# A spectral layer with an MLP: the second product as seven block products, on one core

## The chip, the cores and the metric

One Trainium2 chip, one of its cores. The metric is device microseconds from the start to the end of one execution. TensorE multiplies matrices into PSUM (eight banks), VectorE (DVE), ScalarE (ACT) and GpSimd (POOL) work element by element, SyncE (SP) and ScalarE issue the DMAs.

## What is computed

Eight sequences of 3008 tokens with 256 features pass through a Fourier layer and then through an MLP. Cut to what matters:

```
X  = rfft(x, axis=1)
Yr = Xr @ w_r - Xi @ w_i + b_r ;  Yi = Xr @ w_i + Xi @ w_r + b_i
soft threshold of both by 0.01
y  = irfft(Y)                                # 24064 tokens of 256 features
h  = y @ w_in                                # 256 -> 2048
g  = maximum(0.01 * h, h)                    # leaky relu
out = g @ w_out                              # 2048 -> 256
```

The MLP's weights arrive as float64. Their products are to be more accurate than a single pass of TensorE on the rounded type (float32r) gives, so each operand is split in a high and a low part, and a product is three matmuls: high x high, low x high, high x low.

## The kernel before

The transform length is 47 x 64. A batch passes through `fwd` (transform over n1, its result goes through DRAM as u_dram), `mid` (transform over n2 in `stage_b`, projection in `proj`, threshold, inverse over k2 in `stage_g`, result through DRAM as v_dram), and then, chunk by chunk, `inverse` (over k1) and the MLP. A chunk is two of the 8 x 13 (batch, s) sets and has up to 470 tokens; there are 52. For each chunk and each f (16 blocks of 128 of the 2048 hidden features) there is one step:

- `moe_h(ci, f)`: 6 matmuls of 470 columns (2 halves of the 256 features x 3 parts) into a psh bank (L76, the helper `products`); then L401 ACT 0.01 h into gf, L402 DVE maximum, L403 ACT copy to the high part gh, L404 DVE low part gl.
- `moe_o(ci, f)`: for each of two halves of the output 3 matmuls of 470 columns with w_out as the stationary operand, accumulated over the 16 f in a pso bank (L420). At the last f, L426 ACT copies the result to ob and SP writes it to DRAM.

`moe` writes the order: step f's first product, then the second product of the step three earlier (LAG = 3); v_load of the next chunk at f = 4, its inverse at f = 10 and 12. After each step the generators of `mid` for the next batch and `fwd` for the third after are advanced in proportion, so that they end at three quarters of a batch. The framework then orders the instructions of each engine by its own timeline, starting from that order, and sets the semaphores; tiles with one tag share their buffers, and one that finds none free waits for the release of an older one.

Before the MLP starts there is a prologue: `fwd` of three batches and `mid` of the first in plain float32, and `load_mlp`, which turns the float64 weights into high and low parts in 16 pieces of 512 elements per partition (8 of w_in, 8 of w_out). The last five pieces use buffers that the MLP doesn't need. PSUM: psh 2 banks, psf (transforms) 3, pso 3.

Of the kernel before, what the change touches and what calls it, by code (L numbers as in the profile page):

```python
# [10 lines left out]
U32 = mybir.dt.uint32  # L11
# [13 lines left out]
# High words of float64 numbers, read as float32: the last that float32 holds, and the one that becomes zero.  # L25
# [5 lines left out]
def spectral_mlp_kernel(  # L31
# [23 lines left out]
    NT = 2 * NG * N1  # L55
    CS = 512
    LAG = 3
    # Batches whose first stage runs before the MLP starts, without splitting its operands.
# [11 lines left out]
    def products(dst, pairs):  # L70
        """dst = sum of lhsT.T @ rhs over pairs of operands, each float32 or two parts of it."""
# [25 lines left out]
    def load_weights():  # L97
        """w_r, w_i - w_r and -(w_r + w_i)."""
        r = sb.tile([P, NH, D], F32, name="w_r", tag="yh")
        d = sb.tile([P, NH, D], F32, name="w_d", tag="yl")  # L100
        n = sb.tile([P, NH, D], F32, name="w_n", tag="gl", bufs=LAG + 1)
        i = sb.tile([P, NH, D], F32, name="w_i", tag="c", bufs=1)
# [13 lines left out]
    def float64_parts(src, dh, dl, tags):  # L116
# [3 lines left out]
        raw = sb.tile([P, CS, 2], U32, name="raw", tag=tags[0][0], bufs=tags[0][1])  # L120
# [3 lines left out]
        a = sb.tile([P, CS], F32, name="cva", tag=tags[1])  # L124
        q = sb.tile([P, CS], F32, name="cvq", tag=tags[2])
# [8 lines left out]
        av, qv = (t.rearrange("p (a f) -> p a f", a=na) for t in (a, q))  # L134
        act.copy(dh, av)
        pool.tensor_sub(av, av, dh.bitcast(F32))
        pool.tensor_add(dl, av, qv)

    def load_mlp():
        """Piece by piece; the last ones stay off the buffers that the MLP needs."""  # L140
        ih, il = pair("win", [P, NH, DF])
        oh, ol = pair("wout", [P, NF, D])
        iv, ov = (w.bitcast(U32).rearrange("(a p) f -> p a f", p=P) for w in (w_in, w_out))
        n = CS // NH
        pieces = []
        for c in range(DF // n):
            s = slice(c * n, (c + 1) * n)
            pieces.append((iv[:, :, 2 * c * n:2 * (c + 1) * n], ih[:, :, s], il[:, :, s]))
        n = CS // D
        for c in range(NF // n):  # L150
            s = slice(c * n, (c + 1) * n)
            pieces.append((ov[:, s, :], oh[:, s, :], ol[:, s, :]))
        for i, p in enumerate(pieces):
            early = i < len(pieces) - 5
            float64_parts(*p, (
                ("vin", 2) if early and i % 3 else ("raw", 1),
                ("xh", "xl")[i % 2] if early else "xh",
                ("ob", "gf")[i % 2] if early else "xl",
            ))
            yield 1  # L160

# [1 line left out]
    u_dram = {}  # L163
    first = []
    v_dram = {}
# [65 lines left out]
    def mid(b):  # L231
# [96 lines left out]
        for j in range(2):  # L328
            load(j)
# [288 lines left out]
```

## Time and profile before

| | before |
|---|---|
| median of 3 runs | 2721.57 us (2718.25 to 2722.91) |
| span of the profiled execution, first to last instruction | 2717.4 us |
| mean granted TensorE clock | 0.994 |
| TensorE busy, matmuls | 2662.3 us, 13810 |
| VectorE busy | 1818.5 us |
| ScalarE busy | 1407.4 us |
| GpSimd busy | 317.1 us |
| moved by DMA | 164.79 MB |

The profiled execution is given by its span; its time as the runs measure it is not listed apart. A profile line of a group reads: source line, engine, operation, output<-inputs, shapes, count | busy us, mean ns of one | idle time of the engine just before, and what ended it. "psh<-yh,win_hi" is a matmul into psh with win_hi as weights and yh as the moving operand. PEld are the weight loads, which lie beside the matmuls. Matmul durations overlap with one another.

### The profile page before, as it was taken

The numbers are of one execution on the slowest core, as the hardware profiler recorded it, in microseconds if no ns is written. First come the engines' busy times: TensorE is split into PE (matmuls) and PEld (weight loads), VectorE is DVE, ScalarE is ACT, GpSimd is POOL, SyncE is SP. The second block draws the span as 40 slices with busy tenths as digits, with TensorE's granted clock in tenths as the row PEclk, the third lists the DMA queues.
The fourth block names the chain that finished last, engine by engine and source line by source line (L and its number), as shares of the span: only waits on it lengthen the run. The fifth ranks groups of instructions, "written<-read, shape, count | busy, mean of one in ns | idle before, by whom it ended". The sixth has DMA issues, their size and how long they took to land.

```text
span 2717.4 us, 37211 instructions
## 1 busy us (share of the span) xinstructions
PE 2662.3 (98%) x13810; PEld 2376.7 (87%) x13810; DVE 1818.5 (67%) x3236; ACT 1407.4 (52%) x2779; POOL 317.1 (12%) x245
## 2 busy tenths in 40 slices
PE   6789999999999999999999999999999999999999
PEld 3568888988899888998889888999989999899888
DVE  5988776766767676766667766566656666555554
ACT  3455555555555555555555555555545555445454
POOL 3761110111110111110010100000000000000000
PEclk9899999999999999999999999999999999999999
DMA  8642222221221212221221211211111111100000
GB/s 265 193 146 79 70 57 67 63 58 54 59 62 56 60 56 56 78 59 49 64 60 54 65 53 38 63 36 46 41 46 42 38 34 30 41 30 14 15 15 14
DMA packets 122347, 164.79 MB, mean 61 GB/s; under 512 B 13757, under 2 KB 83381, under 8 KB 122165
## 3 DMA queue, kind: packets, MB, share of 16 engines
q1 hardware_dynamic: 78885, 111.27, 13.4%
q10 hardware_dynamic: 43280, 51.14, 7.1%
q8 instruction: 109, 1.79, 0.3%
q14 instruction: 73, 0.60, 0.1%
HBM read 86.59 MB, written 75.76 MB: 60 GB/s over the span
## 4 chain that ended last, share of the span: by engine, by line
PE 92%; DVE 4%; DMA 2%; issue 1%; ACT 1%; SPq 0%; POOL 0%; ACTq 0%; DVEq 0%
PE pso L420 38%; PE psh L76 38%; PE psf L76 10%; PE psf L373 3%; PE psf L258 3%; DVE t L301 1%; DMA u_dram<-xin 1%; DMA xin<-x_dram 0%; DVE t L303 0%; DMA raw<-w_out_dram 0%; DVE cva L129 0%; DVE cva L131 0%; DMA u<-u_dram 0%; DVE cva L130 0%; DVE raw L132 0%
## 5 line engine op out<-in xcount | busy, mean ns | idle before, releaser
L402 DVE TENSOR_TENSOR gf<-gf,psh 128x470 f32<-128x470 f32 (+1 forms) x832 | 529.3, 636 | 416.6 <-ACT gf L401 408.9
L404 DVE TENSOR_TENSOR gl<-gf,gh 128x470 fp32r<-128x470 f32 (+1 forms) x832 | 562.8, 677 | 355.0 <-ACT gh L403 344.7
L401 ACT ACTIVATE gf<-psh 128x470 f32<-128x470 f32 (+1 forms) x832 | 463.5, 557 | 583.8 <-PE psh L76 572.5
L403 ACT CAST gh<-gf 128x470 fp32r<-128x470 f32 (+1 forms) x832 | 482.4, 580 | 469.5 <-DVE gf L402 466.8
L76 PE MATMUL psh<-yh,win_hi 128*128 128x470 f32 (+1 forms) x1664 | 638.1, 383 | 1.2 <-DVE gf L402 0.9
L420 PE MATMUL pso<-gh,wout_lo 128*128 128x470 f32 (+1 forms) x1664 | 619.8, 372 | 0.0
L76 PE MATMUL psh<-yh,win_lo 128*128 128x470 f32 (+1 forms) x1664 | 619.4, 372 | 0.0
L76 PE MATMUL psh<-yl,win_hi 128*128 128x470 f32 (+1 forms) x1664 | 619.0, 372 | 0.1
L420 PE MATMUL pso<-gh,wout_hi 128*128 128x470 f32 (+1 forms) x1664 | 618.1, 372 | 0.0
L420 PE MATMUL pso<-gl,wout_hi 128*128 128x470 f32 (+1 forms) x1664 | 578.8, 375 | 0.0
L76 PEld LDWEIGHTS psh<-yh,win_lo 128*128 128x128 f32 x1664 | 313.4, 188 | 37.2
L420 PEld LDWEIGHTS pso<-gh,wout_lo 128*128 128x128 f32 x1664 | 312.7, 188 | 36.7
L420 PEld LDWEIGHTS pso<-gh,wout_hi 128*128 128x128 f32 x1664 | 313.1, 188 | 34.5
L76 PEld LDWEIGHTS psh<-yh,win_hi 128*128 128x128 f32 x1664 | 314.0, 189 | 33.4 <-DVE gf L402 2.9
L76 PEld LDWEIGHTS psh<-yl,win_hi 128*128 128x128 f32 x1664 | 316.1, 190 | 29.1 <-DVE yl L387 0.4
L420 PEld LDWEIGHTS pso<-gl,wout_hi 128*128 128x128 f32 x1664 | 308.9, 188 | 33.1 <-DVE gl L404 0.2
L293 POOL TENSOR_TENSOR kb<-bias,kc 128x512 f32<-128x512 f32 x84 | 113.0, 1345 | 1482.8 <-ACT kc L292 1318.3
L301 DVE TENSOR_TENSOR t<-psf,kb 64x256 f32<-64x256 f32 x384 | 161.8, 421 | 30.5 <-PE psf L76 26.2
L373 PEld LDWEIGHTS psf<-ga,vin 120*128 120x128 f32 x832 | 119.8, 191 | 10.1 <-DMA vin<-v_dram 2.2
L373 PE MATMUL psf<-ga,vin 120*128 120x128 f32 x832 | 123.4, 274 | 1.2 <-DMA vin<-v_dram 1.2
L189 POOL TENSOR_TENSOR xs<-xin,xin 120x512 f32<-120x512 f32 (+1 forms) x49 | 64.9, 1325 | 472.3 <-DMA xin<-x_dram 218.1
L258 PEld LDWEIGHTS psf<-fb,u 128*128 128x128 f32 x672 | 96.2, 191 | 13.9 <-ACT kc L292 3.5
(110 smaller groups left out, 2610.1 us busy)
## 6 DMA issues: line engine op xcount, KB each, us to landing
u<-u_dram SPq DMA_DIRECT2D x192, 128.0 KB, 2.8
v_dram<-v ACTq DMA_DIRECT2D x192, 128.0 KB, 2.5
xin<-x_dram SPq DMA_DIRECT2D x96, 240.0 KB, 3.1
u_dram<-xin ACTq DMA_DIRECT2D x96, 240.0 KB, 2.4
vin<-v_dram SPq DMA_DIRECT2D x96, 240.0 KB, 3.3
out_dram<-ob SPq DMA_DIRECT2D x88, 235.0 KB, 2.3
raw<-w_in_dram SPq DMA_DIRECT2D x8, 512.0 KB, 5.6
raw<-w_out_dram SPq DMA_DIRECT2D x8, 512.0 KB, 4.8
```

Source lines behind the costliest of these rows:

```text
L76: nc.tensor.matmul(dst, a, b, start=(i == 0), stop=(i == len(terms) - 1))
L189: eng.tensor_add(xs, xa, xb)
L258: nc.tensor.matmul(pv[:, dh, :, i, :], u[:, i, s], fbt[:, 0:k + 2:k + 1, :], start=True, stop=True)
L293: pool.tensor_add(kb, bias, kc.unsqueeze(1).broadcast_to([P, 2, D]))
L301: dve.tensor_add(t[64 * r:64 * (r + 1), i, :], ps_y[s, r * D:(r + 1) * D], kb[s, r, :])
L373: nc.tensor.matmul(py[:, o:o + P], vin[:, c, i, s], consts["ga"][:, c, :], start=True, stop=True)
L401: act.mul(gf[:, :n], ph[:, :n], SLOPE)
L402: dve.tensor_max(gf[:, :n], gf[:, :n], ph[:, :n])
L403: act.copy(gh[:, :n], gf[:, :n])
L404: dve.tensor_sub(gl[:, :n], gf[:, :n], gh[:, :n].bitcast(F32))
L420: nc.tensor.matmul(po[:, :n], a[:, f, s], r[:, :n], start=(f == 0 and j == 0), stop=(f == NF - 1 and j == 2),)
```

## The change

- `_chunks` pairs sets of equal size: 48 chunks of two halves of 235 tokens (padded to 236 columns) and 4 of two halves of 188. The leftover smaller sets of two batches make one chunk.
- A step is now a pair q of two f. The 2 x 2 blocks of g (two f, two halves of the tokens) and of w_out (two f, two halves of the output) are multiplied by seven block products in place of eight. For w_out the combinations are formed once, in the prologue (`load_wout`); for g in each step: 7 blocks g with three differences or sums, and their high and low parts.
- `moe_h` has 2 x 6 matmuls of 472 columns; `moe_o` 7 x 3 of 236. The seven accumulators take half a bank each, 4 banks in one buffer (tag acc); the transforms keep 2 banks (psf).
- The leaky relu is one ScalarE instruction (Prelu) from PSUM in place of one of ScalarE and one of VectorE.
- At a chunk's end the accumulators are copied by ScalarE (four) and VectorE (three), seven GpSimd additions form the four results, and four DMAs write them.
- The lag is one pair. `mid` has two stages of look-ahead in place of three and loads u one ahead. Many buffers are single (eh, el, xh, xl, zh, zl, t, v, vin), those of x two in place of three; the clipped values go to kb. The weight pieces use the buffers of g, gh and gl. `fwd` after the third batch splits and loads a piece after its matmuls, no longer before.

The core of the diff:

```diff
     def load_wout(c):
+        pool.tensor_add(w32, cv[:, 0, :], cv[:, 1, :])
+        a11, a21, a12, a22 = (wv[:, f, e * P:(e + 1) * P] for f in range(2) for e in range(2))
+        dve.scalar_tensor_tensor(s[:, 1], a21, -1.0, a22, ALU.mult, ALU.subtract)
+        dve.tensor_sub(s[:, 2], a11, a21)
+        dve.scalar_tensor_tensor(s[:, 3], s[:, 1], -1.0, a11, ALU.mult, ALU.subtract)
+        dve.tensor_sub(s[:, 0], a12, s[:, 3])
+        act.copy(oh[:, 0:2], wv[:, :, 0:P])
+        act.copy(oh[:, 6], a22)
+        act.copy(oh[:, 2:6], s)
+        pool.tensor_sub(ol[:, 0:2], wv[:, :, 0:P], oh[:, 0:2].bitcast(F32))
+        dve.tensor_sub(ol[:, 6], a22, oh[:, 6].bitcast(F32))
+        dve.tensor_sub(ol[:, 2:6], s, oh[:, 2:6].bitcast(F32))
...
     def moe_h(ci, q):
+        g = sb.tile([P, 7, TP], F32, name="g", tag="g")[:, :, :tp]
+        for i in range(2):
...
+            act.activation(g[:, 1:3] if i else g[:, 0:5:4], ph, AF.Prelu, alpha=SLOPE)
-        act.mul(gf[:, :n], ph[:, :n], SLOPE)
-        dve.tensor_max(gf[:, :n], gf[:, :n], ph[:, :n])
-        act.copy(gh[:, :n], gf[:, :n])
-        dve.tensor_sub(gl[:, :n], gf[:, :n], gh[:, :n].bitcast(F32))
+        act.copy(gh[:, 0:3], g[:, 0:3])
+        dve.tensor_sub(g[:, 3:5], g[:, 0:3:2], g[:, 4:5].broadcast_to([P, 2, tp]))
+        dve.tensor_add(g[:, 5], g[:, 2], g[:, 3])
+        dve.tensor_sub(g[:, 6], g[:, 1], g[:, 5])
+        act.copy(gh[:, 3:7], g[:, 3:7])
+        dve.tensor_sub(gl[:, 0:3], g[:, 0:3], gh[:, 0:3].bitcast(F32))
+        dve.tensor_sub(gl[:, 3:7], g[:, 3:7], gh[:, 3:7].bitcast(F32))
...
     def moe_o(ci, q):
+        if q == 0:
+            acc_t[ci] = ps.tile([P, 8, 256], F32, name="acc", tag="acc", bufs=1)
+        acc = acc_t[ci]
+        for j in range(7):
+            for i, (a, r) in enumerate(((wh, gh), (wl, gh), (wh, gl))):
                 nc.tensor.matmul(
+                    acc[:, j, :tp], a[:, q, j, :], r[:, j, :],
...
+        act.copy(pc[:, 0:4], acc[:, 0:4, :n])
+        dve.tensor_copy(pc[:, 4:7], acc[:, 4:7, :n])
+        for dst, x, y in ((5, 5, 0), (1, 1, 0), (4, 4, 5), (0, 4, 3), (3, 3, 5), (2, 2, 3), (6, 6, 4)):
+            pool.tensor_add(pc[:, dst], pc[:, x], pc[:, y])
+        for j, r in enumerate((1, 2, 6, 0)):
...
+            sync.dma_start(out[s, o:o + n], pc[:, r])
...
     def moe():
+        for i, (ci, q) in enumerate(steps):
+            moe_h(ci, q)
             if ci + 1 < nch:
+                if q == 2:
                     v_load(ci + 1)
+                if q in (5, 6):
+                    inverse(ci + 1, q - 5)
...
+            if i:
+                moe_o(*steps[i - 1])
```

More of the change, by code (lines that the diff above doesn't have):

```diff
@@ L133, in float64_parts @@
         pool.tensor_mul(q, q, wl.bitcast(F32))
[L134 to L137, printed above, removed]
-    def load_mlp():
[L141 to L159, printed above, removed]
+        return cv, raw
@@ L160, in load_mlp @@
+    def load_mlp():
+        pair("win", [P, NH, DF])
+        pair("wout", [P, NQ, 7, P])
+        for c in range(DF * NH // CS):
+            load_win(c)
+            yield 1
+        for c in range(NQ):
+            load_wout(c)
             yield 1
@@ L326, in stage_g @@
                 act.dma_start(vd[c, 2 * j:2 * j + 2, :N2, :].rearrange("k n d -> n k d"), v[c * N2:(c + 1) * N2])
-        for j in range(2):
-            load(j)
+        load(0)
         yield 0
-        for s in range(NPAIR + 2):
-            if s + 2 < NPAIR:
-                load(s + 2)
+        for s in range(NPAIR + 1):
+            if s + 1 < NPAIR:
+                load(s + 1)
+            if s:
+                yield from proj(s - 1)
             if s < NPAIR:
@@ L345, in spectral_mlp_kernel @@
     nch = len(chunks)
-    t0 = [sum(N1 * sum(n for _, _, n in c) for c in chunks[:i]) for i in range(nch + 1)]
-    y_t, v_t, g_t, o_t = {}, {}, {}, {}
+    t0 = [sum(2 * N1 * c[0][2] for c in chunks[:i]) for i in range(nch)]
+    y_t, v_t, g_t, acc_t = {}, {}, {}, {}
+    yf = const.tile([P, 2, TP], F32, name="y")
     def v_load(ci):
-        vin = sb.tile([PA, 2, 2, D], F32, name="vin", tag="vin")
+        vin = sb.tile([PA, 2, 2, D], F32, name="vin", tag="vin", bufs=1)
         (b, s, _), (b1, _, _) = chunks[ci]
@@ L360, in v_load, with columns @@
         v_t[ci] = vin
+    def columns(ci):
+        n = chunks[ci][0][2] * N1
+        return n, n + n % 2
     def inverse(ci, eh):
-        (_, _, n0), (_, _, n1) = chunks[ci]
-        m = n0 + n1
-        ne, n = m * NK1, m * N1
+        m = chunks[ci][0][2]
+        w = m * NK1
+        n, tp = columns(ci)
         vin = v_t[ci]
-        py = bank("psf", 3)
+        py = bank("psf", 2)
         s = slice(eh * P, (eh + 1) * P)
@@ L424, in moe_o @@
-            if f == NF - 1:
-                ob = sb.tile([P, NT], F32, name="ob", tag="ob")
-                act.copy(ob[:, :nt], po[:, :nt])
-                sync.dma_start(out[s, t0[ci]:t0[ci + 1]], ob[:, :nt])
-    steps = [(ci, f) for ci in range(nch) for f in range(NF)]
+                    acc[:, j, :tp], a[:, q, j, :], r[:, j, :],
+                    start=(q == 0 and i == 0 and j % 2 == 0), stop=(q == NQ - 1 and i == 2),
+                    skip_group_check=True,
+                )
+        if q < NQ - 1:
+            return
@@ L431, in moe @@
+    steps = [(ci, q) for ci in range(nch) for q in range(NQ)]
+    home = [c[1][0] for c in chunks]
     def moe():
-        for i, (ci, f) in enumerate(steps):
-            moe_h(ci, f)
-            if i >= LAG:
-                moe_o(*steps[i - LAG])
+        for i, (ci, q) in enumerate(steps):
+            moe_h(ci, q)
             if ci + 1 < nch:
-                if f == 4:
+                if q == 2:
                     v_load(ci + 1)
-                if f in (10, 12):
-                    inverse(ci + 1, (f - 10) // 2)
-            yield 2 * (ci + (f + 1) / NF) / NS
@@ L569, in _chunks, with n2 @@
 def _chunks(nb):
-    sets = [(b, s, NG if (NG - 1) * NS + s < N2 else NG - 1) for b in range(nb) for s in range(NS)]
-    assert len(sets) % 2 == 0
-    return [sets[i:i + 2] for i in range(0, len(sets), 2)]
+    def n2(s):
+        return NG if (NG - 1) * NS + s < N2 else NG - 1
+    full = [s for s in range(NS) if n2(s) == NG]
+    rest = [s for s in range(NS) if n2(s) < NG]
+    assert len(full) % 2 == 0
+    chunks, left = [], []
+    for b in range(nb):
+        chunks += [[(b, s, NG) for s in full[i:i + 2]] for i in range(0, len(full), 2)]
+        left += [(b, s, NG - 1) for s in rest]
+        while len(left) > 1:
+            chunks.append([left.pop(0), left.pop(0)])
+    assert not left
+    return chunks
 def _tokens(nb):
```

188 lines of the change are left out of this document (98 added, 90 removed).

## The prediction

> **What bounds the kernel now.** I read the page from the top: busy shares, then the slices, then the chain that ended last, then TensorE's waits.
>
> ```profile
> PE 2662.3 (98%) x13810; PEld 2376.7 (87%) x13810; DVE 1818.5 (67%) x3236; ACT 1407.4 (52%) x2779; POOL 317.1 (12%) x245
> PE   6789999999999999999999999999999999999999
> PEclk9899999999999999999999999999999999999999
> PE 92%; DVE 4%; DMA 2%; issue 1%; ACT 1%; SPq 0%; POOL 0%; ACTq 0%; DVEq 0%
> PE pso L420 38%; PE psh L76 38%; PE psf L76 10%; PE psf L373 3%; PE psf L258 3%; DVE t L301 1%; DMA u_dram<-xin 1%; DMA xin<-x_dram 0%; DVE t L303 0%; DMA raw<-w_out_dram 0%; DVE cva L129 0%; DVE cva L131 0%; DMA u<-u_dram 0%; DVE cva L130 0%; DVE raw L132 0%
> ```
>
> From the fourth slice on TensorE is full at full clock, and 92% of the chain is TensorE: 38% first product, 38% second. A busy matmul is not yet a dense one, so I look at starts in a steady stretch (start, duration, engine).
>
> ```profile
> 1185.75 0.28 PE L76 MATMUL psf<-wn_hi,eh 128*128 128x256 f32 x1
> ...
> 1186.58 0.38 PE L76 MATMUL psh<-yh,win_hi 128*128 128x470 f32 x1
> ...
> 1187.86 0.35 PE L420 MATMUL pso<-gh,wout_hi 128*128 128x424 f32 x1
> ...
> 1189.02 0.28 PE L76 MATMUL psf<-wd_lo,eh 128*128 128x256 f32 x1
> ...
> 1198.14 0.61 PE L258 MATMUL psf<-fb,u 128*128 128x128 f32 x4
> 1198.50 0.67 PE L420 MATMUL pso<-gl,wout_hi 128*128 128x470 f32 x2
> ```
>
> Seven matmuls of 256 columns take 0.83 us (118.6 ns each), six of 470 take 1.28 (213.3), six of 424 take 1.16 (193.3): a line of 0.4425 ns per column. The 0.38 us durations overlap and are not the price; the spacing is. So TensorE's columns bound the time. Does it wait?
>
> ```profile
> 500.00:800.00 300.00, 300.00 (x1599) 272.38 (x1598) 204.99 (x372) 158.34 (x314) 31.34 (x24) 1.00 0.20 58
> PE psf L76 <- DVE ef L263: 12.3, 4, 4.5
> PE psh L76 <- DVE gf L402: 0.9, 4, 0.4
> ```
>
> In the window (PE, PEld, DVE, ACT, POOL busy) it is busy throughout; of its waits in the whole run (us, times, longest) the longest is on ef, which only the prologue has, and those on VectorE's part of the MLP come to 0.9 us.
>
> **The matmuls removed and added.** Counts:
>
> ```profile
> L76 PE MATMUL psh<-yh,win_lo 128*128 128x470 f32 x1408 | 528.7, 376 | 0.0
> L420 PE MATMUL pso<-gh,wout_lo 128*128 128x470 f32 x1408 | 529.4, 376 | 0.0
> L420 PE MATMUL pso<-gh,wout_lo 128*128 128x424 f32 x256 | 90.4, 353 | 0.0
> ```
>
> Each product has three such groups. Second product before: 4224 x 213.3 + 768 x 193.3 ns = 1049 us. After: 52 chunks of two equal halves (48 of 2 x 236 columns, 4 of 2 x 188), 8 pairs of f each, 7 block products x 3 parts: 8064 matmuls of 236 columns and 672 of 188. The line gives 109.7 ns for 236. For 188 it gives 88, while the nearest lower row (128 columns, four in 0.36 us) shows 90; I take 100 between 90 and 109.7. That is 885 + 67 = 952 us: a gain of 97. The first product goes to 4608 x 214.2 + 384 x 171.9 ns = 1053 from 1049: a loss of 4. **TensorE: -94 us.** Its bounds: the shortest row, 90 ns for all, would give -259; the next longer row, 118.6, gives -9.
>
> The rule to weigh here: the Trainium skill, "TensorE: Matmul & The Clock Gate", section "LDWEIGHTS (loading the stationary operand)", says that a weight load lasts its columns over 1.2 GHz, 107 ns for 128, whatever the contraction. It speaks against the change, which has 21 loads where there were 12. By it 236 columns would still be just above the load, and 188 would stand at 107, which makes the sum 5 us worse, an estimate from that page. No row here shows this type of operand under 256 columns, so the trace can't decide it.
>
> **ScalarE and VectorE per pair of f.**
>
> ```profile
> L404 DVE TENSOR_TENSOR gl<-gf,gh 128x470 fp32r<-128x470 f32 x704 | 484.0, 688 | 303.7 <-ACT gh L403 294.0 <-PE pso L420 2.0 <-PE psh L76 1.3
> L402 DVE TENSOR_TENSOR gf<-gf,psh 128x470 f32<-128x470 f32 x704 | 453.2, 644 | 358.8 <-ACT gf L401 352.8
> L403 ACT CAST gh<-gf 128x470 fp32r<-128x470 f32 x704 | 412.8, 586 | 403.8 <-DVE gf L402 401.4 <-issue 1.3 <-ACT xin L208 0.4
> L401 ACT ACTIVATE gf<-psh 128x470 f32<-128x470 f32 x704 | 396.4, 563 | 505.3 <-PE psh L76 497.5 <-ACT v L324 1.4 <-ACT yh L386 0.9
> L272 DVE TENSOR_TENSOR el<-psf,eh 128x512 fp32r<-128x512 f32 x84 | 57.2, 681 | 0.0
> L380 DVE TENSOR_TENSOR y<-psf,odd 128x240 f32<-128x240 f32 x88 | 35.5, 404 | 5.8 <-ACT odd L379 4.5
> L379 ACT COPY odd<-psf 128x240 f32<-128x240 f32 x88 | 31.5, 358 | 14.9 <-PE psf L373 13.4 <-DVE y L382 0.2
> ```
>
> VectorE's line is (681 - 404)/272 = 1.02 ns per element. Before: 2 x (688 + 644) = 2.66 us. After: differences of 472, 236, 236, 708 and 944 elements, 0.64 + 0.40 + 0.40 + 0.88 + 1.12 = 3.44 us. VectorE's total: 1818 - 416 x 2.66 + 416 x 3.44 + 52 x 0.88 (its three accumulators) = 2190 us. ScalarE's slope is (563 - 358)/230 = 0.89 ns; two leaky relus at 563, copies of 708 and 944 at 586 + 212 and 586 + 422 ns: 2.93 us against 2.30, total near 1670. Both are under TensorE's new 2570, so they cost nothing as sums. What they cover with is time between need and use, and that shrinks: the lag was three f, five half-steps of 6 x 213 = 1.28 us, or 6.4 us, for a chain of 563 + 644 + 586 + 688 ns = 2.5 us. Now it is one pair: from the end of one first product to its second product lie the second product before (21 x 109.7 = 2.3 us) and the next first product (2.57 us): 4.9 us, some 1.4 of the transforms on either side in most of the run (2717 - 164 us from the first MLP matmul, shown below, less 2098 for both products leave 1.1 per pair, bunched into three quarters of a batch), and 1 us more until the fourth block product. The chain is leaky relu 0.56, three combinations 1.44, copy of four 1.01, low parts of four 1.12: 4.1 us, and 0.88 for the low parts of three ahead of the last. Five us against six to nine: covered, but whatever VectorE does for the transforms in that time comes on top.
>
> What can take the cover away is GpSimd, which gets seven additions per chunk.
>
> ```profile
> L189 POOL TENSOR_TENSOR xs<-xin,xin 120x256 f32<-120x256 f32 x7 | 5.3, 754 | 52.3 <-DMA xin<-x_dram 35.8 <-ACT gh L403 12.2 <-DVE gf L402 4.3
> L301 DVE TENSOR_TENSOR t<-psf,kb 64x256 f32<-64x256 f32 x52 | 21.9, 420 | 1.6 <-PE psf L76 1.0
> L303 DVE TENSOR_TENSOR t<-t,c 128x512 f32<-128x512 f32 x13 | 18.5, 1424 | 0.1
> ...
> L301 DVE TENSOR_TENSOR t<-psf,kb 64x256 f32<-64x256 f32 x324 | 136.6, 421 | 28.9 <-PE psf L76 25.3
> ...
> L303 DVE TENSOR_TENSOR t<-t,c 128x512 f32<-128x512 f32 x81 | 55.7, 688 | 1.2
> ```
>
> The L301 and L303 rows stand once for the first 164 us, where GpSimd works beside, and once for 230 to 2700 us. The difference of two SBUF operands (L303) took 1424 ns against 688; the sum with a PSUM operand stays at 420. All five new VectorE operations have two SBUF operands. 7 x 0.75 = 5.3 us of GpSimd per chunk could thus double 2.6 us of VectorE: 52 x 2.6 = 137 us more on VectorE at most, still below TensorE in sum, but in one burst on the pair after a chunk's end. The Trainium skill, "GPSIMD Engine Reference", section "Key points", states that contention for operations with two SBUF inputs; by that rule, the trace agrees.
>
> Stalls: at least 0, as now (VectorE held TensorE in the steady state for under 1 us). At most I take half a microsecond in each of 273 busy pairs: 137. **I put 30 us**: about 0.4 us in each chunk's turn (20), and 10 elsewhere, nearer the rows of now, for the sums leave room.
>
> Other parts: the accumulators (one buffer of four banks) are read by ScalarE (940 elements, about 0.98 us) and VectorE (0.88) while the next chunk's second first product runs (2.57 us): 0. Two banks instead of three for the transforms, single buffers for eh, el, xh, xl, zh, zl, t, vin: their units are spread over the pairs, some three pairs to a k1 pair, so chains of 3 to 5 us have twice that; 0, or in the 30. An x piece now waits, on SyncE's queue, for the DMA that empties its buffer, and u and vin loads queue behind it:
>
> ```profile
> u<-u_dram SPq DMA_DIRECT2D x192, 128.0 KB, 2.8
> vin<-v_dram SPq DMA_DIRECT2D x96, 240.0 KB, 3.3
> ```
>
> They land in about 3 us, and vin is issued three pairs (2553/416 = 6.1 us each) ahead: 0; if that cover goes, TensorE waits at the inverse. Output DMAs double in number and halve in size: hidden but for the last.
>
> **The prologue.**
>
> ```profile
> 164.02 0.76 PE L76 MATMUL psh<-yh,win_hi 128*128 128x470 f32 x1 [0.31 <-ACT xin L208]
> 201.21 1.61 POOL L137 TENSOR_TENSOR wout_lo<-cva,cvq 128x512 fp32r<-128x512 f32 x1
> 100.00:125.00 25.00, 18.05 (x69) 11.61 (x67) 24.57 (x35) 12.84 (x26) 16.09 (x13) 0.93 0.71 200
> 150.00:175.00 25.00, 17.23 (x74) 13.03 (x75) 18.94 (x33) 13.84 (x30) 18.03 (x14) 0.93 0.78 231
> ```
>
> Before, the MLP began at 164 us while the last weight pieces ran until 201. After, its g buffers are those of the pieces, so it begins when the last but one is done. VectorE was full there (24.57 of 25 us) and gets eight pieces with four combinations and two low parts more, about 1.9 us each, 15 in all. More buffers for the raw pieces pull the other way. At most the overlap of 37 us and 15 are lost, at least nothing: **+25**, the middle.
>
> **The tail.**
>
> ```profile
> 2713.43 0.93 ACT L426 COPY ob<-pso 128x423 f32<-128x423 f32 x2 [1.49 <-PE pso L420]
> ```
>
> This 0.93 becomes one copy as long plus seven GpSimd additions, 5.3 us, and the last pair waits for its chain: 4.1 less the second product before it, 2.3. **+8** (5 to 12).
>
> **Sum.** -94 + 30 + 25 + 8 = -31 on the span of 2717.4 us gives 2686. The median of the runs, 2721.57, stands 4.2 above that span, so 2691 us, 1.1% less.
>
> **The rivals.**
> - Slower: the second product of each pair waits for the low parts of its combinations, since one pair of lag is too short beside VectorE's transforms. For it: 3.44 us of VectorE per pair, GpSimd's doubling. Against it: 2190 of 2690 us in sum. From 61/416 = 0.15 us per pair it eats the gain; at 0.25 us (104 in place of 30) it gives 2765.
> - Nothing hidden costs: stalls and prologue 0: 2717.4 - 94 + 8 + 4 = 2636. For it: no wait of now in the steady state.
> - The shorter matmuls don't come closer than those of 256 columns, 118.6 ns: TensorE gains 9, and the time is 2776. Or, worse, they fall to the rate of the plain type, of which L258 has two records per matmul: the four in 0.36 us are two matmuls, 180 ns for 128 columns, so some 330 for 236, 8736 x 220 ns more, about 4600 us. Nothing from 256 columns up hints at it.
> - The leaky relu needs another function table than the copies:
>
> ```profile
> 1.92 1.28 ACT L94 ACT_TABLE_LOAD   x1 [1.92 <-POOL zero L236]
> ```
>
> Now there is one load, 1.28 us. Two for each of 416 pairs are 1065 us on ScalarE: 1670 becomes 2735, a new bound near 2900. The Trainium skill, "ScalarE: Activation LUTs", section "Table sets: the hidden batching unit", says that cheap functions lie in every set, and does not list this one.
>
> **How the numbers follow.** Forecast (2645 to 2716): 0.50. All hidden: 0.10. Slower by the chain: 0.24. The 118.6 ns floor: 0.07. Plain rate or tables: 0.05. The rest, 0.04, is within 0.2% (5.4 us, what can be told from no change here; a run of now lies up to 3.3 from the median); the chain at just its break-even adds 0.02 to that, out of its own. Faster 0.60, same 0.06, slower 0.34. The range leaves out the last case, part of all-hidden and the chain's far end: 2645 to 2790; the likeliest's own is 2645 to 2716.
>
> **What would show it.** Second-product matmuls 110 ns apart (256 columns: 118.6); first products at 214; the wait of the second product for VectorE's low parts, near 30 us in sum; first MLP matmul at about 190 us; VectorE near 2200 us busy, more if GpSimd's additions stretch the 944-element differences beyond 1.12 us; one or two table loads. The prediction is wrong if that spacing is above 115, or if TensorE has over 60 us of new idle time after 230 us.

## The result, and the profile after

| | before | after |
|---|---|---|
| median | 2721.90 us (4 runs, 2718.25 to 2722.91) | 2751.20 us (4 runs, 2749.43 to 2751.63) |
| span of the profiled execution | 2717.4 us | 2749.7 us |
| first matmul of the MLP starts | 164.0 us | 206.4 us |
| from there to the start of the last second-product matmul | 2549 us | 2535 us |
| from that to the end | 4.2 us | 8.3 us |

The ratio after to before is 1.0111, 95% interval 1.0097 to 1.0126: slower by 1.1%, where 1.1% faster was forecast. The last three rows, from the start times of the matmuls in the two traces, sort the difference of the spans: +42 ahead of the MLP, -14 in it, +4 behind it, which makes +32. One execution of s2_no_additions and one of p7_all_relieved below were slow ones, of 13716 and 4106 us; they are counted in the medians of the table of runs and not in the ratios.

The page of the kernel after: busy us (share, count), two rows of its 40 slices in tenths, and the shares of the chain that ended last.

```profile
PE 2628.6 (96%) x17554; PEld 2415.1 (88%) x17554; DVE 2342.0 (85%) x3737; ACT 1602.5 (58%) x2743; POOL 683.7 (25%) x609
PE   6659999999999999999999999999999999999998
DVE  5998998889888999889888899888888889877776
PE 67%; DVE 24%; issue 3%; ACT 3%; DMA 2%; POOL 1%; ACTq 0%; SPq 0%; DVEq 0%; POOLq 0%
```

The chain says what the busy line hides: 24% of the time on the chain that ended last is VectorE's, against 4% before. And the third slice of PE (137 to 206 us) has fallen from 8 to 5: the MLP hasn't begun. Three windows of the same trace (start and end, length, then PE, PEld, DVE, ACT and POOL busy, clock, DMA share, GB/s):

```profile
150.00:175.00 25.00, 15.90 (x63) 10.38 (x61) 23.92 (x38) 10.72 (x22) 13.98 (x13) 0.93 0.69 197
175.00:200.00 25.00, 6.17 (x28) 4.79 (x28) 23.55 (x40) 9.45 (x23) 14.33 (x12) 0.68 0.18 50
500.00:800.00 300.00, 293.04 (x1993) 272.05 (x1992) 265.85 (x423) 177.57 (x305) 81.23 (x68) 1.00 0.21 59
```

From 175 to 200 TensorE works 6 of 25 us, VectorE is full and the DMA engines are nearly idle (0.18). In the steady stretch TensorE, which was busy for 300.00 of 300, is idle for 7, with VectorE at 266 (205 before) and GpSimd at 81 (31). What it waits for from 250 us on (total us, times, longest); before, this view has no row at all there:

```profile
PE psf L76 <- DVE zl L333: 9.3, 9, 2.0
PE acc L441 <- DVE gl L428: 6.0, 11, 1.3
PE acc L441 <- DVE gl L427: 4.5, 7, 1.0
PE psh L76 <- ACT g L419: 2.8, 2, 1.4
```

L428 and L427 are the low parts of the combinations, zl is the low part of the thresholded spectrum, so all but the last are VectorE's last step of a chain. All waits of this view together come to 32 us; those for gl, the low parts that the second product needs, are 10.5 of them. The new instructions of the MLP by group (us busy, mean ns):

```profile
L428 DVE TENSOR_TENSOR gl<-g,gh 128x944 fp32r<-128x944 f32 (+1 forms) x416 | 488.1, 1174 | 192.4 <-ACT gh L426 190.6
L419 ACT ACTIVATE g<-psh 128x472 f32<-128x472 f32 (+1 forms) x832 | 454.4, 557 | 308.3 <-PE psh L76 241.7
L452 POOL TENSOR_TENSOR pc<-pc 128x235 f32<-128x235 f32 (+1 forms) x364 | 336.0, 934 | 872.2 <-ACT pc L449 783.6
```

The leaky relu costs 557 ns in the mean, as the scaling by 0.01 in its place did (L401 of before, 557), and the trace has one table load as before. The spacing of the matmuls, in the steady stretch:

```profile
1188.92 0.38 PE L76 MATMUL psh<-yh,win_lo 128*128 128x472 f32 x1
...
1189.56 0.38 PE L76 MATMUL psh<-yh,win_lo 128*128 128x472 f32 x1
...
1191.20 0.27 PE L441 MATMUL acc<-gh,wout_hi 128*128 128x236 f32 x1
...
1193.55 0.28 PE L441 MATMUL acc<-gh,wout_hi 128*128 128x236 f32 x1
```

Three steps of 472 columns take 0.64 us (213 ns each; the median of all is 215), and 21 steps of 236 columns take 2.35 us: 112 ns, where 109.7 was put. The matmuls of 188 columns have the same median, 112, where 100 was put.

### The profile page after: what moved, and what is told of

Its sections match the earlier page's. It is cut to its first block, busy times and chain, and to the rows that moved or that the text cites. A ratio compares the mean times of both kernels' runs of the same rounds, so it can differ in the third digit from the quotient of the medians.

```text
span 2749.7 us, 45619 instructions
## 1 busy us (share of the span) xinstructions
PE 2628.6 (96%) x17554; PEld 2415.1 (88%) x17554; DVE 2342.0 (85%) x3737; ACT 1602.5 (58%) x2743; POOL 683.7 (25%) x609
## 4 chain that ended last, share of the span: by engine, by line
PE 67%; DVE 24%; issue 3%; ACT 3%; DMA 2%; POOL 1%; ACTq 0%; SPq 0%; DVEq 0%; POOLq 0%
PE psh L76 28%; PE acc L441 27%; PE psf L76 7%; DVE gl L427 3%; DVE gl L428 3%; PE psf L394 3%; DVE t L318 3%; DVE g L423 3%; PE psf L276 2%; DVE g L424 2%; DVE t L320 1%; DVE zl L333 1%; DVE g L425 1%; DVE kb L319 1%; ACT gh L426 1%
## 5 line engine op out<-in xcount | busy, mean ns | idle before, releaser
L441 PE MATMUL acc<-gl,wout_hi 128*128 128x236 f32 (+1 forms) x2912 | 806.9, 277 | 11.3 <-DVE gl L428 6.0
L441 PE MATMUL acc<-gh,wout_hi 128*128 128x236 f32 (+1 forms) x2912 | 806.4, 277 | 3.4 <-ACT gh L426 1.8
L441 PE MATMUL acc<-gh,wout_lo 128*128 128x236 f32 (+1 forms) x2912 | 800.4, 275 | 0.0
L428 DVE TENSOR_TENSOR gl<-g,gh 128x944 fp32r<-128x944 f32 (+1 forms) x416 | 488.1, 1174 | 192.4 <-ACT gh L426 190.6
L76 PE MATMUL psh<-yh,win_hi 128*128 128x472 f32 (+1 forms) x1664 | 628.0, 378 | 2.8 <-ACT g L419 2.8
L76 PE MATMUL psh<-yl,win_hi 128*128 128x472 f32 (+1 forms) x1664 | 623.3, 375 | 0.0
L76 PE MATMUL psh<-yh,win_lo 128*128 128x472 f32 (+1 forms) x1664 | 621.4, 373 | 0.0
L441 PEld LDWEIGHTS acc<-gl,wout_hi 128*128 128x128 f32 x2912 | 555.8, 191 | 25.5 <-DVE gl L428 12.3
L441 PEld LDWEIGHTS acc<-gh,wout_hi 128*128 128x128 f32 x2912 | 554.7, 190 | 21.2 <-DVE pc L450 3.3
L441 PEld LDWEIGHTS acc<-gh,wout_lo 128*128 128x128 f32 x2912 | 555.4, 191 | 10.2
L452 POOL TENSOR_TENSOR pc<-pc 128x235 f32<-128x235 f32 (+1 forms) x364 | 336.0, 934 | 872.2 <-ACT pc L449 783.6
L427 DVE TENSOR_TENSOR gl<-g,gh 128x708 fp32r<-128x708 f32 (+1 forms) x416 | 395.0, 950 | 10.8 <-ACT gh L422 9.2
L423 DVE TENSOR_TENSOR g<-g 128x472 f32<-128x472 f32 (+1 forms) x416 | 316.0, 760 | 103.6 <-ACT g L419 101.9
L311 POOL TENSOR_TENSOR kb<-bias,kc 128x512 f32<-128x512 f32 x84 | 141.3, 1682 | 884.6 <-ACT kc L310 817.2
L425 DVE TENSOR_TENSOR g<-g 128x236 f32<-128x236 f32 (+1 forms) x416 | 194.0, 466 | 3.0
```

Source lines behind the costliest of these rows:

```text
L76: nc.tensor.matmul(dst, a, b, start=(i == 0), stop=(i == len(terms) - 1))
L311: pool.tensor_add(kb, bias, kc.unsqueeze(1).broadcast_to([P, 2, D]))
L423: dve.tensor_sub(g[:, 3:5], g[:, 0:3:2], g[:, 4:5].broadcast_to([P, 2, tp]))
L425: dve.tensor_sub(g[:, 6], g[:, 1], g[:, 5])
L427: dve.tensor_sub(gl[:, 0:3], g[:, 0:3], gh[:, 0:3].bitcast(F32))
L428: dve.tensor_sub(gl[:, 3:7], g[:, 3:7], gh[:, 3:7].bitcast(F32))
```

## The experiments

Three theories, one for each place. (1) The stalls in the MLP come from GpSimd's additions, which either stretch VectorE's operations or keep other GpSimd work waiting. (2) The MLP begins late because VectorE's work on the weight pieces grew; rivals are the order of the buffers, the shallower look-ahead of the first `mid`, and GpSimd's folds, which slow VectorE. (3) 112 ns is the load of 128 columns of weights, and no shorter moving operand goes below it; the rival is a cost per column with a larger constant. Each kernel is after.py with the edit shown, unless said otherwise. All times:

| kernel | median us | ratio to before, 95% |
|---|---|---|
| after | 2751.20 | 1.0111 [1.0097, 1.0126] |
| s1_dve_additions | 2708.81 | 0.9958 [0.9945, 0.9970] |
| s2_no_additions | 2700.33 | 0.9923 [0.9910, 0.9937] |
| s3_kb_on_dve | 2743.81 | 1.0086 [1.0072, 1.0100] |
| e1_shapes | 2687.4 (one time) | |
| b1_prelu_in_before (on before.py) | 2720.32 | 0.9999 [0.9991, 1.0008] |
| p1_mid0_three_stages | 2744.46 | 1.0092 [1.0076, 1.0107] |
| p2_no_weight_combinations | 2745.30 | 1.0092 [1.0078, 1.0106] |
| p3_last_pieces_apart | 2748.19 | 1.0101 [1.0088, 1.0115] |
| p4_both (p1 and p3) | 2739.72 | 1.0071 [1.0058, 1.0083] |
| p5_both_no_combinations (p4 and p2) | 2732.11 | 1.0042 [1.0027, 1.0057] |
| p6_no_gpsimd_folds | 2734.48 | 1.0045 [1.0028, 1.0063] |
| p7_all_relieved (p5 and p6) | 2726.25 | 1.0019 [1.0009, 1.0029] |
| v1_all (p4 and s1) | 2699.45 | 0.9926 [0.9912, 0.9939] |
| v2_two_before (v1, one batch less ahead) | 2697.58 | 0.9916 [0.9901, 0.9930] |

**s1_dve_additions: the chunk's additions on VectorE.**

```diff
-        for dst, x, y in ((5, 5, 0), (1, 1, 0), (4, 4, 5), (0, 4, 3), (3, 3, 5), (2, 2, 3), (6, 6, 4)):
-            pool.tensor_add(pc[:, dst], pc[:, x], pc[:, y])
+        b0 = pc[:, 0:1].broadcast_to([P, 2, n])
+        dve.tensor_add(pc[:, 1:6:4], pc[:, 1:6:4], b0)
+        dve.tensor_add(pc[:, 4], pc[:, 4], pc[:, 5])
+        dve.tensor_add(pc[:, 0], pc[:, 4], pc[:, 3])
+        dve.tensor_add(pc[:, 3], pc[:, 3], pc[:, 5])
+        dve.tensor_add(pc[:, 2:7:4], pc[:, 2:7:4], pc[:, 3:5])
```

> The seven additions at a chunk's end go from GpSimd to VectorE, as five operations of 470, 235, 235, 235 and 470 elements. Theory 1 (GpSimd's additions stretch VectorE's operations and hold back the kb additions queued behind them; this makes the stalls of the second to fourth pair of a chunk): most of the stalls after 250 us go, 30 to 45 us, and VectorE's busy time falls although it has more to do; about 2712 us. Rival (a lag of one pair is too short by itself): VectorE gets 2 us more per chunk, stalls stay or grow; 2751 to 2770 us.

2708.81 us: 42 less than after, and below before. The MLP begins when it did (205.9 us), so nearly all of it came out of the stalls; the end behind the last matmul is 1 us shorter. The steady window and the waits from 250 us on, of this kernel:

```profile
500.00:800.00 300.00, 299.64 (x2059) 280.28 (x2058) 264.96 (x469) 183.89 (x317) 49.37 (x26) 1.00 0.22 61
PE psf L76 <- DVE el L290: 2.9, 5, 0.8
PE psh L76 <- ACT g L419: 1.4, 4, 0.5
PE acc L441 <- DVE gl L428: 1.1, 2, 0.5
```

VectorE has more instructions (469 against 423) and is busy no longer than in after (264.96 against 265.85 us): what it took over, it saved by being slowed less. TensorE is back to 299.64 of 300. The same group, first of after, then of this kernel, from 250 to 2700 us:

```profile
L423 DVE TENSOR_TENSOR g<-g 128x472 f32<-128x472 f32 x376 | 292.4, 778 | 84.0 <-ACT g L419 82.8
```

```profile
L423 DVE TENSOR_TENSOR g<-g 128x472 f32<-128x472 f32 x377 | 265.1, 703 | 88.3 <-ACT g L419 86.2
```

The mean hides where it falls. The median is nearly the same, 647 and 643 ns; the additions come in one burst per chunk. From 250 us on I sum, over the steps from one matmul to the next that last over 50 ns longer than the median of their shape, the time above that median: 26 us before (where the view of waits is empty, so this is the level of the count without stalls), 79 after and 37 here. The 42 us between the last two are s1's gain. Of after's 79, 54 lie in the second to fourth pairs of a chunk, where 356 of the 364 additions run; the same part of the chunk has 10 in before.

**s2_no_additions: the same additions left out.**

```diff
-        for dst, x, y in ((5, 5, 0), (1, 1, 0), (4, 4, 5), (0, 4, 3), (3, 3, 5), (2, 2, 3), (6, 6, 4)):
-            pool.tensor_add(pc[:, dst], pc[:, x], pc[:, y])
```

> The seven additions are left out: four of the accumulators are written as they are. Theory 1 (GpSimd's additions make the stalls): as with the additions on VectorE or up to 5 us better, plus about 5 us at the end where the last additions stood; about 2705 us. Rival (lag of one pair): 2746 us, only the end is shorter.

2700.33 us: 51 less than after, of which 3 come from the shorter end (8.3 us behind the last matmul in after, 5.2 here). On GpSimd the additions cost about 51 us, on VectorE about 9.

**s3_kb_on_dve: stretch or queue?** GpSimd has another duty in `proj`, the addition L311 for the threshold's bounds; it could be late because it stands behind the chunk's additions in GpSimd's queue, which would make zl late. Here it moves to VectorE, and the additions stay.

```diff
-                    pool.tensor_add(kb, bias, kc.unsqueeze(1).broadcast_to([P, 2, D]))
+                    dve.tensor_add(kb, bias, kc.unsqueeze(1).broadcast_to([P, 2, D]))
```

> The chunk's additions stay on GpSimd; only the kb additions of mid (84, which wait in GpSimd's queue behind them) go to VectorE. Theory 1a (the queue: kb comes late, so t, z and stage_g come late): the waits for zh and zl, 21 us in the changed kernel, go; 15 to 25 us less, about 2731 us. Theory 1b (GpSimd's additions stretch VectorE's own operations): VectorE gets 0.7 us more per k1 pair and its differences stay stretched; 0 to 8 us less or slower, 2743 to 2758 us.

2743.81 us, 7 less; TensorE's wait for zl is 7.8 us where it was 9.3. The 15 to 25 us of the queue don't come; at most these 7 are its share, and an operation less on GpSimd would by itself slow VectorE less. Most of the stalls stay with the additions.

**e1_shapes: what sets the spacing.** Three chunks of four multiply only part of their block: 128 columns of the moving operand, or 64 columns of weights, or both (pair 0 stays whole). It leaves that part of the second product out.

```diff
+                w, k = ((P, tp), (P, 128), (64, tp), (64, 128))[ci % 4 if q else 0]
-                    acc[:, j, :tp], a[:, q, j, :], r[:, j, :],
+                    acc[:w, j, :k], a[:, q, j, :w], r[:, j, :k],
```

> From the second pair of a chunk on, the second product's matmuls have another shape in three of four chunks: 128 columns of the moving operand in place of 236; 64 weight columns in place of 128; both. The other columns of the accumulators are left as the first pair wrote them. Theory 3 (a floor that goes with the weight load of 128 columns): spacing 112 ns with 236 and with 128 columns, about 105 to 110 (the columns' line, 109.7) with 64 weight columns, and about 60 with both. Rival a (a floor per matmul whatever its shape): 112 ns in all four. Rival b (columns only, 188 being an exception): about 62 ns in both chunks of 128 columns.

The starts of its matmuls, first with 128 columns of weights and 128 of the moving operand, then with 64 and 128:

```profile
500.85 0.28 PE L442 MATMUL acc<-gh,wout_lo 128*128 128x128 f32 x1
...
501.63 0.27 PE L442 MATMUL acc<-gl,wout_hi 128*128 128x128 f32 x1
```

```profile
378.99 0.23 PE L442 MATMUL acc<-gh,wout_lo 128*64 128x128 f32 x1
...
379.42 0.22 PE L442 MATMUL acc<-gl,wout_hi 128*64 128x128 f32 x1
```

Seven steps take 0.78 us (111 ns) and 0.43 us (61 ns). The medians over the run: 112 ns for 128 weight columns with 236, 188 or 128 moving columns alike; for 64 weight columns 108 with 236, 87 with 188, 60 with 128. So a step lasts as long as the longer of two terms, one that goes with the moving columns and one that goes with the weight columns, and the second is 112 ns for 128. Theory 3 holds. That this second term is the load itself is the reading that fits; the run varies the weight columns, and the load has no row of its own with 112 ns (it is recorded as some 190). The rule that the prediction weighed, of the Trainium skill's page "TensorE: Matmul & The Clock Gate", section "LDWEIGHTS (loading the stationary operand)", gives 107 ns for a load of 128 columns; the measured 112 is 5 above and decides.

**b1_prelu_in_before: the leaky relu alone, in before.py.**

```diff
-        act.mul(gf[:, :n], ph[:, :n], SLOPE)
-        dve.tensor_max(gf[:, :n], gf[:, :n], ph[:, :n])
+        act.activation(gf[:, :n], ph[:, :n], AF.Prelu, alpha=SLOPE)
```

> The kernel before with only the leaky relu changed: one ScalarE instruction in place of one of ScalarE and one of VectorE. Both theories of the change: VectorE loses 529 us of busy time, TensorE stays the bound; 0 to 8 us less than before (2714 to 2722 us), the gain in the prologue alone. A second function table would show as loads and a time far above.

0.9999 [0.9991, 1.0008]: no difference, though VectorE's busy time falls by 489 us (from 1818.5 to 1329.5). VectorE wasn't the bound of before. The group that does it now:

```profile
L401 ACT ACTIVATE gf<-psh 128x470 f32<-128x470 f32 (+1 forms) x832 | 463.5, 557 | 855.2 <-PE psh L76 801.1 <-issue 27.8 <-PE pso L419 16.4
```

**The prologue.** First what VectorE does in it: the weight pieces' groups of after, 0 to 206 us.

```profile
L130 DVE SCALAR_TENSOR_TENSOR cv<-raw,cv 128x512 uint32<-128x512 uint32 x16 | 16.9, 1059 | 0.3
...
L157 DVE SCALAR_TENSOR_TENSOR cv<-cv 128x128 f32<-128x128 f32 x8 | 6.6, 820 | 0.0
L156 DVE TENSOR_TENSOR cv<-cv 128x128 f32<-128x128 f32 x8 | 6.5, 814 | 0.0
...
L164 DVE TENSOR_TENSOR wout_lo<-cv,wout_hi 128x512 fp32r<-128x512 f32 x8 | 5.5, 683 | 0.1
L155 DVE SCALAR_TENSOR_TENSOR cv<-cv 128x128 f32<-128x128 f32 x8 | 5.3, 663 | 0.0
...
L158 DVE TENSOR_TENSOR cv<-cv 128x128 f32<-128x128 f32 x8 | 3.9, 487 | 0.2
L163 DVE TENSOR_TENSOR wout_lo<-cv,wout_hi 128x128 fp32r<-128x128 f32 x8 | 2.2, 281 | 0.0
```

The four combinations and two low parts (L155 to L164) come to 30 us, twice the 15 that were put. An operation of 128 elements takes 820, 814 or 663 ns in the mean. Its single instructions (start, us):

```profile
175.08 1.35 DVE L155 SCALAR_TENSOR_TENSOR cv<-cv 128x128 f32<-128x128 f32 x1
176.35 1.35 DVE L156 TENSOR_TENSOR cv<-cv 128x128 f32<-128x128 f32 x1
177.62 0.81 DVE L157 SCALAR_TENSOR_TENSOR cv<-cv 128x128 f32<-128x128 f32 x1
...
200.15 0.29 DVE L155 SCALAR_TENSOR_TENSOR cv<-cv 128x128 f32<-128x128 f32 x1
200.35 0.28 DVE L156 TENSOR_TENSOR cv<-cv 128x128 f32<-128x128 f32 x1
```

The same line takes 0.28 us and 1.35. What GpSimd does beside them (it is idle from 198.4 to 201.0):

```profile
174.57 1.71 POOL L151 TENSOR_TENSOR cv<-cv 128x512 f32<-128x512 f32 x1
176.24 1.31 POOL L204 TENSOR_TENSOR xin<-xin,xin 120x512 f32<-120x512 f32 x1
177.51 0.77 POOL L162 TENSOR_TENSOR wout_lo<-cv,wout_hi 128x256 fp32r<-128x256 f32 x1
```

The two operations of 1.35 us lie beside GpSimd operations of 512 elements, the one of 0.81 beside one of 256, those of 0.28 beside none. This holds for the whole trace. Of the 2208 operations of L155 to L158, L320, L423 to L425, L427 and L428, all with two SBUF operands, 327 last over 0.06 us longer than the median of their shape with GpSimd idle, and every one of the 327 has a GpSimd operation beside it. The extra is at most 0.50 us beside an addition of 235 elements (L452) and at most 1.12 beside 512 elements.

The start itself, first in after, then in before:

```profile
200.70 0.79 PE L76 MATMUL psf<-zh,gb_hi 128*128 128x512 f32 x1 [10.78 <-ACT zh L332]
201.29 1.91 PE L394 MATMUL psf<-ga,vin 120*128 120x128 f32 x8
...
206.44 0.59 PE L76 MATMUL psh<-yh,win_hi 128*128 128x472 f32 x2
```

```profile
153.93 0.71 PE L373 MATMUL psf<-ga,vin 120*128 120x128 f32 x4
...
210.50 0.47 PE L76 MATMUL psf<-zh,gb_hi 128*128 128x512 f32 x1 [0.82 <-DVE t L301]
```

zh is made from the second batch on, so this is the second batch's `mid`. With two stages of look-ahead its first inverse over k2 stands ahead of the first chunk's inverse (L394) in TensorE's order, and TensorE waits 10.8 us for it, while the chunk's vin is issued at 187.1 us and takes 3 to land. In before, with three stages, that product comes 46 us after the MLP's start. The other part is the first `mid`: its last product comes at 176.2 us, at 145.2 in before. No run below gives the second batch its third stage back; in each of them TensorE waits 3.4 to 11.6 us at this place.

**p2_no_weight_combinations.** Four plain blocks stand where the combinations were; the combinations are left out.

```diff
-        dve.scalar_tensor_tensor(s[:, 1], a21, -1.0, a22, ALU.mult, ALU.subtract)
-        dve.tensor_sub(s[:, 2], a11, a21)
-        dve.scalar_tensor_tensor(s[:, 3], s[:, 1], -1.0, a11, ALU.mult, ALU.subtract)
-        dve.tensor_sub(s[:, 0], a12, s[:, 3])
```

> The four combinations of w_out's blocks per piece are left out of the prologue (32 VectorE operations, 22 us busy in the changed kernel); all else is the same. Theory 2 (the MLP starts 42 us later because VectorE, full in the prologue, has these operations to do, stretched by GpSimd): the first MLP matmul comes 15 to 22 us earlier than 206 us, and the time falls as much, to about 2732 us. Rival (the shallower look-ahead of the first batch's mid is what is late): no change, 2748 to 2752 us.

2745.30, only 6 less: a miss. The first MLP matmul comes at 201.3 (206.4 in after), although VectorE from 175 to 200 us is down from 23.55 to 17.98 us: it wasn't the only thing that the start waited for.

**p3_last_pieces_apart.** The last five pieces of w_out get buffers of their own, as before.

```diff
-        raw = sb.tile([P, CS, 2], U32, name="raw", tag=("gh", "gl")[n % 2])
+        raw = sb.tile([P, CS, 2], U32, name="raw", tag="raw" if late else ("gh", "gl")[n % 2], bufs=1 if late else 2)
-        cv = sb.tile([P, 3, CS], F32, name="cv", tag="g")
+        cv = sb.tile([P, 3, CS], F32, name="cv", tag="pc" if late else "g", bufs=1 if late else 2)
```

> The last five pieces of w_out use a raw buffer of their own and the buffer of the chunk's end (pc) in place of those of g, gh and gl, one at a time. Theory 2b (the MLP must wait until the pieces leave its buffers, and the pieces compete with its first inverse on VectorE): the first MLP matmul at 165 to 185 us, and 20 to 35 us less, about 2723 us. Rival (VectorE's work of the prologue, or the first batch's mid, sets the start wherever the pieces lie): first MLP matmul still at 195 us or later, or it starts earlier and then waits for weights; 2740 to 2752 us.

2748.19, 3 less: a miss. The MLP begins at 198, but then shares VectorE with the pieces until 263 us.

**p1_mid0_three_stages.** The first `mid` gets back its third stage and u its third buffer.

```diff
+        if b == 0:
+            load(1)
+            for s in range(NPAIR + 2):
+                if s + 2 < NPAIR:
+                    load(s + 2)
+                if s < NPAIR:
+                    stage_b(s)
+                    yield 16 * P
+                if 0 <= s - 1 < NPAIR:
+                    yield from proj(s - 1)
+                if 0 <= s - 2 < NPAIR:
+                    stage_g(s - 2)
+                    yield 3 * CS
+            return
```

> The first batch's mid gets its order of before back (three stages of look-ahead, u loaded two ahead, three u buffers); nothing else changes. Theory 2 (VectorE's work sets the start of the MLP): 0 to 8 us less, 2743 to 2751 us, since VectorE stays full. Rival (the shallower look-ahead is what is late: the last zf was at 176 us against 145): the first MLP matmul comes 20 to 31 us earlier, about 2725 us.

2744.46, 7 less. The first `mid` ends 24 us earlier (152 us in place of 176) and the first product begins at 185, but the second only at 208.7 (215.4 in after). The wait, in the same trace:

```profile
ACT g L433 <- DVE wout_lo L164: 3.9, 1, 3.9
```

The leaky relu's g waits for a weight piece to release the buffer that they share. Hence the next one.

**p4_both: p1 and p3 together.** The edits are those two, but the third buffer of u is t's:

```diff
-            u = sb.tile([P, 2, D], F32, name="u", tag="u", bufs=2)
+            third = b == 0 and j % 3 == 2
+            u = sb.tile([P, 2, D], F32, name="u", tag="t" if third else "u", bufs=1 if third else 2)
```

> Both edits that alone gave 7 and 3 us: the first batch's mid with three stages of look-ahead (its third u buffer is that of t, idle in that batch), and the last five pieces of w_out in buffers of their own. Theory 2c (two gates in series: the mid of the first batch decides when the first product can start, the pieces in the MLP's buffers decide when its leaky relu can; lifting one leaves the other): the first second-product matmul at 185 to 195 us (215 in the changed kernel, 209 with either edit alone), and 20 to 30 us less, about 2726 us. Rival (VectorE's sum of work in the prologue is the bound, whatever the order): no more than the sum of the two, 10 us, about 2741 us.

2739.72, 11 less, hardly more than the sum of the parts (10). First product at 179, first second product at 191.5; then VectorE is nearly full until the pieces end at 267 us, and TensorE works 44.95 of the 50 us from 250 on (49.11 in after). Time moved from one side of the MLP's start to the other.

**p5_both_no_combinations: p4 without the combinations.** The edits are p4's and p2's; the combinations are left out.

> Both edits of the prologue, and the four combinations of w_out's blocks per piece left out. Theory 2d (VectorE's sum of work is the bound of the prologue, so that reordering alone gave 11 us): with the order no longer in the way the 22 us of combinations count nearly in full; 15 to 22 us less than with both edits alone, about 2721 us. Rival (GpSimd's and the DMAs' pace of the pieces sets it): as with both edits, 2735 to 2740 us.

2732.11: 8 less than p4, half of the lower end expected.

**p6_no_gpsimd_folds.** For the second and third batch GpSimd's sums and differences of x ahead of the MLP are left out, and the plain halves go in.

```diff
+            if 1 <= b < NPRE:
+                s_t[c] = [(xa,), (xb,)]
+                return
```

> The changed kernel with GpSimd's sums and differences of x (28 operations of 1.3 us in the prologue) left out for the second and third batch: their first stage runs on x itself. Theory 2e (VectorE's operations of the prologue are stretched by GpSimd, 56 us of 171 before the MLP's start): the stretch falls by 10 to 20 us and the MLP starts as much earlier; about 2736 us. Rival (VectorE's own work and the order alone): 2746 to 2752 us.

2734.48, 17 less, the most of any single edit in the prologue, with not one VectorE instruction taken away. The first MLP matmul comes at 192.7 us instead of 206.4, the first second-product matmul at 202.6 instead of 215.4. The time of VectorE's operations above the shortest of their kind in the first 215 us falls from 56 to 37 us. The edit also takes the folds out of GpSimd's queue, in which weight pieces stand, and out of TensorE's inputs; these shares aren't told apart.

**p7_all_relieved: p5 and p6 together**, all of it left out that they leave out.

> The changed kernel with everything taken from the prologue that the single edits took: the mid transform of the first batch in three stages as before, the last weight pieces in buffers of their own, no combinations of weight blocks (four plain blocks used in their place), and no GpSimd folds for the batches that are transformed ahead (their halves go in plain). It leaves out that work; the MLP is unchanged. Single edits took 7, 3, 6 and 17 us off 2751. Theory: VectorE's work and stretching ahead of the MLP, and the order of the buffers, are the whole of the later start, and the reliefs add up: 33 us off, about 2718 us, first matmul of the second product near 180 us. Rival: a chain of transfers of the first batch sets the start once VectorE is relieved, so the reliefs don't add: 2728 us or more, and VectorE has idle time from 150 us to the first inverse.

2726.25 us, 25 less than after: between the two theories, so the reliefs add up for the most part (33 would be all). The first MLP matmul comes at 176, 12 us later than before, the first second product at 186, 16 later. Two windows and two of the largest rows among the waits from 120 to 178 us:

```profile
125.00:150.00 25.00, 20.04 (x82) 13.59 (x82) 16.41 (x34) 13.31 (x30) 3.54 (x4) 0.98 0.68 193
150.00:175.00 25.00, 11.97 (x46) 10.31 (x47) 17.32 (x30) 9.26 (x22) 14.57 (x12) 0.50 0.40 124
POOL cv L132 <- DVE raw L131: 26.9, 3, 20.0
PE psf L76 <- ACT zh L332: 8.3, 1, 8.3
```

VectorE has 8 us to spare in each 25 now, as the rival has it. The first `mid` is no longer late: its last product comes at 146.3 us (145.2 in before). The 8.3 us for zh are the second batch's first inverse over k2 again. The first chunk's vin is issued at 154.6 us and lands 3 to 4 us later, and its inverse comes at 168.9, right behind that product. By this trace most of the 12 us are there; a run that moves the product is missing. That the pieces wait on one another (the first row) doesn't show at the start.

**v1_all: p1, p3 and s1, nothing left out.**

> Both edits of the prologue, and the chunk's additions on VectorE (which gave 42 us alone). If the two causes are independent: 2709 us less what the prologue's pair gives; by theory 2c about 2684 us, by its rival about 2699 us.

2699.45 us, ratio 0.9926 [0.9912, 0.9939]: faster than both kernels. s1 and p4 add up: 42 and 11 make 53, and 52 are gone.

**v2_two_before: v1 with two batches transformed ahead in place of three.**

```diff
-    NPRE = 3
+    NPRE = 2
```

> v1 (three mid stages, last pieces apart, the chunk's seven additions as five VectorE operations) with two batches transformed ahead of the MLP in place of three: the forward transform of the third runs beside the MLP. Theory: VectorE's sum ahead of the MLP sets its start, so 14 folds and their splits less there give about 7 us: 2692 us, against 2699 for v1. Rival: the same splits take VectorE beside the first batch of the MLP, where it already has the last weight pieces until 267 us, and the gain comes back as waits of the second product for low parts: 2697 to 2705.

2697.58 us; its interval overlaps v1's. The time is the rival's, but not its mechanism. Counted from 0, the second product of pair 100 (of 416) starts 15.3 us earlier than in v1 (816.8 and 832.1), and of pair 200 15.6 earlier; of pair 300 only 4.5. The gain is paid back late, where the last forward transform now runs. The matmuls of one kind from 1650 to 2050 us, v1 and then v2:

```profile
L76 PE MATMUL psf<-xh,fa_hi 120*120 120x512 f32 x3 | 1.2, 395 | 0.0
```

```profile
L76 PE MATMUL psf<-xh,fa_hi 120*120 120x512 f32 x14 | 5.5, 396 | 0.0
```

Eleven more of each of three kinds, at 234 ns between starts, are 7.7 us of TensorE, which had nothing to spare there; in the prologue the same transform runs where TensorE has idle time.

## Why the prediction was wrong

The sum was -94 + 30 + 25 + 8 = -31. Measured, by its own terms: -63 + 49 + 42 + 4 = +32. No term had the wrong sign; three were mis-sized, all to the same side, and together they turn it.

- **TensorE: -94, measured -63.** The failed step is "the line gives 109.7 ns for 236", and 100 for 188. The line from 470, 424 and 256 columns was carried below its last row, where for 128 columns of weights it stops (for 64 it goes on, 108 and 87 ns in e1): 112 ns for both, 8736 x 112 = 978 us in place of 952. The rest is the first product, 215 ns and not 214.2, 172 for 376 columns: 8 us lost in place of 4. e1_shapes shows the floor. The bound at its slow side, 118.6, did hold the value.
- **Stalls: 30, measured 49** (what is left of the MLP's -14 when -63 is taken off). The cause stands as told: additions on GpSimd lengthen VectorE's operations with two SBUF operands in a burst, and the pairs after a chunk's end pay. s1 takes 42 us out. The mis-sized step is "0.4 us in each chunk's turn": the 54 us in the second to fourth pairs, less the 10 of before, make 0.8 us per chunk. The burst takes 7 x 0.93 us, where 0.75 each was put, so it lasts into a second pair, and GpSimd's other work follows it. Where the waits fall was only in part as told: not "near 30 us" at the second product for the low parts, but 10.5 us there, and the largest row, 9.3 us, at zl of the transforms. And the extra isn't a doubling: it goes with the GpSimd operation beside, up to 0.50 us for 235 elements, whatever VectorE's own length.
- **The prologue: 25, measured 42.** That the MLP would wait for the pieces was foreseen, and their extra work put at 15 us, with durations of an undisturbed VectorE. It took 30. The step that failed is that the stretching, worked out for the MLP from rows of this very stretch of time (1424 ns against 688), wasn't applied to the work added in it. And the two stages of `mid` have no term in this sum, though the first `mid` ends 31 us later (176.2 against 145.2) and the second batch's first product makes TensorE wait 10.8 us in front of the first chunk. The middle between nothing and 52 was taken where p1, p3, p6 and the trace show several causes in a row: the first `mid` is shallower, the second `mid` stands in front of the first inverse, the pieces hold g's buffers, GpSimd's folds are in the way.
- **The tail: 8, measured 4.** From the last second-product matmul to the end 8.3 us, 4.2 before.
- **What was put at nothing** stayed so as far as the waits tell: from 250 us on none is for a DMA, so x pieces on SyncE's queue and more output DMAs cost nothing there. Of the waits on the transforms, among which the single buffers would show, 3 us for el are left in s1; the 9.3 for zl go with the additions. VectorE's total was 2342, not 2190, and still below TensorE's. The leaky relu as forecast: 557 ns and no second table load, so that rival is out.
- **The rivals.** "Slower by the chain" came closest by its result, not its size: 49/416 = 0.12 us per pair is below its point of decision, 0.15. The rival of the 118.6 ns floor had the spacing as its cause, at 85 us of loss where 31 were measured; no rival had the prologue. That is the flaw of the case list: the middle values were taken as if independent. VectorE, 85% busy over the run and 94% from 175 to 200 us, with GpSimd beside it, is a likely reason why two of them erred the same way. Neither sign of being wrong came: the spacing is below 115 ns, and TensorE's new idle time from 230 us on is 33 us, below 60. Both left out the start, where the first MLP matmul came at 206 us and not at about 190.

Shown by runs: the floor (e1), the additions (s1, s2, and s3 against most of the queue), and for the prologue 25 us of time (p7, whose first MLP matmul comes 30 of the 42 us earlier). Read from traces alone: the second batch's product ahead of the first inverse, and that each lengthened VectorE operation of the ten lines has a GpSimd operation beside it. Open: how the prologue's loss divides among its causes.

## What to carry to other kernels

Before making matmuls shorter, look whether the columns still take longer than the load of their weights: the gain of seven products for eight was cut from 97 to 71 us by 2 to 12 ns on each of 8736. Work is not off the path because it is put on an idle engine: additions on GpSimd cost about 51 us, the same on the busier VectorE about 9. When look-ahead is shortened, read what now stands ahead of the first use in each engine's order. Cost the work added to a stretch with the durations of that stretch, not with the best ones of the run.

## What the runs showed of the hardware that was not expected

- Matmuls of float32r with 128 columns of weights start 112 ns apart at 236, 188 and 128 moving columns; with 64 weight columns 60 ns at 128. The weight load alone is recorded as 190 ns, the matmul as 275; neither is the price.
- A VectorE operation of 128 x 128 with two SBUF operands took 0.28 us alone, 0.81 beside a GpSimd operation of 256 elements and 1.35 beside ones of 512. What comes on top goes with the GpSimd operation's length (at most 0.50 us for 235 elements, 1.12 for 512) and not with VectorE's, so small VectorE operations suffer most in proportion.
- The parametric relu on ScalarE takes 563 ns for 128 x 472 from PSUM, as the scaling of 128 x 470 did (563), and the trace has one table load, as before.
